# Padded copies of K for three of four segments: on-chip DMA copies of the live rows in place of VectorE multiplies, with new engine orders

## The chip, the cores and the metric

The kernel runs on one core of a Trainium2 chip. The metric is the device time of one execution in microseconds (us); lower is better. The kernel before took 261.88 us (median of three runs, 261.73 to 261.92).

## The reference, cut to what matters

One input x (2048 tokens of 512 features, bfloat16) goes through two branches that a gate mixes:

```
g   = sigmoid(sum(x * gate_w))            # one number for each token
a   = attention branch of x               # below
b   = (gelu(x @ w_gate) * (x @ w_up)) @ w_down      # inner width 1792
out = g * a + (1 - g) * b
```

The attention branch has 32 heads of width 16 and cuts the tokens into 4 segments of 512. In each segment q, k and v are x times a weight. Causal softmax attention runs inside the segment: exp(q.k / 4) with a mask, times v, divided by the row's sum. To this comes a memory read from all earlier segments: phi(q) M / (phi(q) z), where phi(t) is t + 1 for positive t and exp(t) otherwise; M sums phi(k) v and z sums phi(k) over the earlier segments. A gate per head (beta) mixes memory and attention, and wo projects the result.

## The kernel before, in words

All work is cut by segment, s = 0 to 3. K and Q are held transposed, features on the 128 partitions: `kT` and `qT` have 4 tiles of 128 features (8 heads of 16 rows each) by 512 tokens. TensorE multiplies row groups of 32 partitions, and a group of 32 holds two heads. To get the scores of one head alone, the stationary operand must be K with the other head's 16 rows set to zero. That is what `kpad[0]` and `kpad[1]` are: K with the odd, or the even, 16-row blocks of every 32 set to zero. `klow` holds pieces of K in a third layout, for the blocks at the diagonal.

Work of a segment, by task name (s is the segment, t a tile of features or of tokens):

- `K`, `Q`, `V` (tasks K1_0.0 and so on): projections on TensorE in pieces of two matmuls of 512 columns; `K1_0ev` and the like copy the result out of PSUM, on ScalarE or VectorE.
- `kp` (line 776 for segment 0, line 785 for segments 1 to 3): fills kpad from kT by a multiply with a 0/1 column on VectorE. Segments 1 to 3 have four such tasks each, `kp1_00` to `kp1_11`, each of two tiles for one j.
- `kl`: fills klow, on VectorE or ScalarE.
- `qk` (line 920): scores. For each t there are A0 and B0, which read kpad[0], A1 and B1, which read kpad[1], and for even t a block L, which reads klow. All write the same four PSUM banks X (`psXALL`), so the next one can start only when `exp` (line 926, ScalarE, 128 x 2048) has read X. GpSimd masks the result (`msk`, line 929).
- `pv` (lines 968 and 976): probabilities times V, and `pvt`, `norm` on VectorE.
- `pk` (lines 744 to 749): phi of K, written over kT in place, then `pkT`, a DMA transpose of it; `mz` (line 886) adds to the memory. `numx`, `num`, `numd`, `nump`: the memory read of a segment, whose result goes by the DMA transposes `oTd` (line 574) to oT. numx writes the X banks too, so qk of that segment waits for the last `nump`.
- `G`, `U`: gate and up projections; `gelu` (ScalarE); `Um` (line 1067): product on VectorE; `D` and `R` (line 1088): down projection and wo, the R pieces cut in four row groups; `fin`, `out`: scale and store.

TensorE runs in three ways: the whole array (line 541), four column groups of 32 (line 543, 968, 976, 886), or four row groups of 32 (lines 920, 1088, 839). A projection matmul in a stretch of the order that also has a pv task is issued as four matmuls of 32 columns (line 543) instead of one (line 541).

Each of the five queues runs its tasks strictly in the order written out in `ORDER` at the top of the file, one string for each engine; SyncE's string (`sp`) has all DMAs but the first few weights, in issue order. An emitter puts a semaphore wait in front of an instruction for each earlier writer or reader of what it touches. A waiting instruction holds all that stand behind it in its queue. The DMA helper at line 574 issues transposes, line 578 plain copies. The weights w_wu, w_wd and w_wo and the x tiles of segment 2 are held back by ticks of segment 0's exp.

The buffers that matter here: there is one kT and one pair kpad for all segments. kpad[j] of segment s may be filled only when the last qk of segment s-1 that reads it is done; phi of K writes kT, so it comes after whatever reads kT.

Of the kernel before, what the change touches and what calls it, by code (L numbers as in the profile page):

```python
# [7 lines left out]
PE, ACT, DVE, POOL, SP = "pe", "act", "dve", "pool", "sp"  # L8
# [5 lines left out]
ALU = mybir.AluOpType  # L14
# [427 lines left out]
def mm_t(n):  # L442
    return max(0.026, n / 2363.0)


def act_t(n, psum=True, ap=False):
    return (0.167 if psum else 0.20) + n / 1200.0 + (0.093 if ap else 0.0)
# [814 lines left out]
```

## Time and profile before

| | before |
|---|---|
| median of 3 runs | 261.88 us |
| profiled execution | 262.03 us, of which the span of the program 260.8 us |
| TensorE busy | 254.2 us (97%) |
| ScalarE busy | 212.4 us (81%) |
| VectorE busy | 183.8 us (70%) |
| GpSimd busy | 104.8 us (40%) |
| bytes moved by DMA | 18.43 MB |

The span runs from the first to the last instruction of the program. PE is TensorE (PEld its weight loads), DVE is VectorE, ACT ScalarE, POOL GpSimd, SP SyncE, and SPq SP's issue of DMAs. Busy is the union of an engine's instructions; a TensorE matmul overlaps the next, so that busy does not say how closely they are packed. L785 is line 785 of the file. "a <- b" in a list of waits reads: a waited until b let it go. A timeline row has its start, its length, the engine, the line, the operation and the number of instructions merged into it; "32*128" are the rows and columns of the array that a matmul uses.

### The profile page before, as it was taken

The numbers are of one execution on the slowest core, as the hardware profiler recorded it, in microseconds if no ns is written. First come the engines' busy times: TensorE is split into PE (matmuls) and PEld (weight loads), VectorE is DVE, ScalarE is ACT, GpSimd is POOL, SyncE is SP. The second block draws the span as 40 slices with busy tenths as digits, with TensorE's granted clock in tenths as the row PEclk, the third lists the DMA queues.
The fourth block names the chain that finished last, engine by engine and source line by source line (L and its number), as shares of the span: only waits on it lengthen the run. The fifth ranks groups of instructions, "written<-read, shape, count | busy, mean of one in ns | idle before, by whom it ended". The sixth has DMA issues, their size and how long they took to land.

```text
span 260.8 us, 10396 instructions
## 1 busy us (share of the span) xinstructions
PE 254.2 (97%) x4653; PEld 126.9 (49%) x4674; DVE 183.8 (70%) x348; ACT 212.4 (81%) x191; POOL 104.8 (40%) x260
## 2 busy tenths in 40 slices
PE   8999999999999999999999999999999999999996
PEld 3544354444553664534454563544455445454454
DVE  0688789989997616989889307899898301598563
ACT  4699899899999969988849867889988878877722
POOL 8206484878000544193800008548310128526430
DMA  7963263069049022190005303020000300320002
GB/s 217 318 173 61 45 186 103 3 213 195 3 49 238 14 53 63 23 124 3 3 3 120 64 5 92 15 85 1 3 4 14 93 5 0 85 64 3 3 3 83
DMA packets 32780, 18.43 MB, mean 71 GB/s; under 512 B 20576, under 2 KB 32736, under 8 KB 32736
## 3 DMA queue, kind: packets, MB, share of 16 engines
q1 hardware_dynamic: 31904, 16.99, 27.8%
q8 instruction: 36, 0.59, 0.9%
q10 hardware_dynamic: 832, 0.79, 0.9%
q14 instruction: 8, 0.07, 0.1%
HBM read 9.84 MB, written 2.10 MB: 46 GB/s over the span
## 4 chain that ended last, share of the span: by engine, by line
PE 89%; DVE 4%; ACT 2%; DMA 1%; issue 1%; POOL 0%; ACTq 0%
PE psW L541 33%; PE psW L543 24%; PE psW L1088 14%; PE psXALL L920 8%; PE psW L968 5%; PE psXALL L543 2%; DMA hT<-in_A_x_dram 1%; PE psXALL L541 1%; ACT pt L926 1%; DVE hT L564 1%; PE psW L976 1%; DVE tb L982 1%; ACT ptl L926 1%; PE psXALL L839 1%; DVE glog L814 0%
## 5 line engine op out<-in xcount | busy, mean ns | idle before, releaser
L926 ACT ACTIVATE pt<-psXALL 128x2048 bf16<-128x2048 f32 x64 | 120.1, 1877 | 25.7 <-PE psXALL L920 23.0
L929 POOL TENSOR_SCALAR_AFFINE_SELECT pt<-pt 128x256 bf16<-128x256 bf16 x128 | 57.5, 461 | 82.9 <-ACT pt L926 77.8
L929 POOL TENSOR_SCALAR_AFFINE_SELECT ptl<-ptl 128x512 bf16<-128x512 bf16 x32 | 23.1, 721 | 52.7 <-ACT ptl L926 51.0
L1067 DVE TENSOR_TENSOR hT<-psW,hT 128x512 bf16<-128x512 f32 x56 | 36.9, 682 | 9.0 <-PE psW L541 7.8
L1088 PE MATMUL psW<-wd,hT 32*128 32x512 bf16 x576 | 34.8, 374 | 0.0
L982 DVE STREAM_TRANSPOSE tb<-psW 128x512 f32<-128x512 f32 x32 | 22.3, 706 | 9.9 <-PE psW L976 9.8
L541 PE MATMUL psW<-xT,wu 128*128 128x512 bf16 x111 | 28.1, 380 | 1.2 <-issue 0.8
L1117 DVE TENSOR_SCALAR ost<-psW,omgt 128x512 bf16<-128x512 f32 x8 | 5.8, 747 | 32.7 <-PE psW L541 31.1
L541 PE MATMUL psW<-xT,wg 128*128 128x512 bf16 x112 | 28.0, 380 | 0.6 <-issue 0.3
L920 PE MATMUL psXALL<-qT,kpad 32*128 32x320 bf16 (+3 forms) x512 | 25.6, 272 | 0.4 <-ACT ptl L926 0.2
L543 PE MATMUL psW<-xT,wu 128*32 128x512 bf16 x424 | 25.9, 379 | 0.0
L543 PE MATMUL psW<-xT,wg 128*32 128x512 bf16 x432 | 25.4, 379 | 0.0
L1088 PEld LDWEIGHTS psW<-wd,hT 32*128 32x128 bf16 x576 | 18.9, 93 | 10.4
L1051 ACT ACTIVATE hT<-psW 128x512 bf16<-128x512 f32 x28 | 15.5, 596 | 6.5 <-PE psW L543 6.0
L920 PEld LDWEIGHTS psXALL<-qT,kpad 32*128 32x128 bf16 x512 | 8.8, 92 | 22.1 <-ACT pt L926 16.0
L968 PE MATMUL psW<-pt,vaug 128*17 128x192 bf16 (+3 forms) x512 | 19.2, 273 | 0.0
L541 PEld LDWEIGHTS psW<-xT,wu 128*128 128x128 bf16 x118 | 10.5, 98 | 13.6 <-issue 1.2
L541 PEld LDWEIGHTS psW<-xT,wg 128*128 128x128 bf16 x116 | 10.5, 98 | 13.0 <-issue 1.9
L968 PEld LDWEIGHTS psW<-pt,vaug 128*17 128x17 bf16 x512 | 11.8, 91 | 9.5 <-issue 0.8
L543 PEld LDWEIGHTS psW<-xT,wu 128*32 128x32 bf16 x424 | 10.9, 97 | 10.3 <-issue 0.4
L926 ACT ACTIVATE ptl<-psXALL 128x2048 bf16<-128x2048 f32 x8 | 15.0, 1880 | 1.0 <-PE psXALL L920 0.8
L543 PEld LDWEIGHTS psW<-xT,wg 128*32 128x32 bf16 x432 | 10.6, 97 | 10.1 <-issue 0.4
(124 smaller groups left out, 385.4 us busy)
## 6 DMA issues: line engine op xcount, KB each, us to landing
out_dram<-ost SPq DMA_DIRECT2D x15, 128.0 KB, 1.8
wg<-in_B_w_gate_dram SPq DMA_DIRECT2D x2, 896.0 KB, 7.2
wu<-in_B_w_up_dram SPq DMA_DIRECT2D x2, 896.0 KB, 6.8
wd<-in_B_w_down_dram SPq DMA_DIRECT2D x2, 896.0 KB, 5.9
phkt<-in_A_x_dram SPq DMA_DIRECT2D x3, 512.0 KB, 4.5
vlow<-vaug SPq DMA_DIRECT2D x8, 136.0 KB, 2.9
hT<-in_A_x_dram SPq DMA_DIRECT2D x2, 256.0 KB, 4.0
wo<-in_A_wo_dram SPq DMA_DIRECT2D x1, 512.0 KB, 6.2
```

The source lines that it names most:

```text
L541: return e.matmul(view(), lhsT, rhs, start=first, stop=last)
L543: r = e.matmul(view()[c:c + 32, :], lhsT[:, c:c + 32], rhs, start=first, stop=last, tile_position=(0, c))
L564: alts[DVE] = [Instr(lambda e: e.tensor_copy(dst(), src()), reads=reads, writes=writes, est=dve_t(n))]
L920: instrs.append(Instr(lambda e, g=g, lhs=lhs, rhs=rhs, c0=c0, ncol=ncol: e.matmul(X[g][:, c0:c0 + ncol], lhs(32 * g), rhs(32 * g), start=T ...
L926: exp_task(s, f"exp{s}_{t}{name}", [Instr(lambda e: e.activation(dst[:], XALL[:, :].rearrange("p (g c) -> p g c", g=4), ACTF.Exp, scale=AT ...
L929: task(f"msk{s}_{t}{name}", POOL, [Instr(lambda e, view=view, pat=pat, base=base: e.affine_select(out=view, in_=view, compare_op=ALU.is_ge ...
L968: instrs.append(Instr(lambda e, t=t, q=q, kb=kb, slot=slot, c0=c0: e.matmul(gp.f32()[32 * q:32 * q + 17, 128 * kb + 64:512], Vaug[sl][:, k ...
L982: task(f"pvt{s}_{t}_{j}", DVE, [Instr(lambda e: e.transpose(Tb[:, j, :], gp.f32()[:, :]), [gp.key], [("Tb", j)], 0.71)], grp=gp)
L1051: lambda e, g=g, ft=ft, s=s: e.activation(hT[s % 2][:, ft, :], g.f32()[:, :], ACTF.Gelu_apprx_tanh),
L1067: task(f"Um{s}_{ft}", DVE, [Instr(lambda e, g=g, ft=ft: e.tensor_tensor(hT[sl][:, ft, :], g.f32()[:, :], hT[sl][:, ft, :], ALU.mult), [g.k ...
L1088: return Instr(lambda e: e.matmul(gs[tile].f32()[:, :], a[32 * r:32 * r + 32, :], b[32 * r:32 * r + 32, :], start=False, stop=False, tile_ ...
L1117: DVE: [Instr(lambda e: e.tensor_scalar(ost[:], g.f32()[:, :], omgt[:, gt:gt + 1], None, ALU.mult), rd, wr, dve_t(512, ap=True))]}, grp=g))
```

## The change

Segments 1 to 3 no longer fill kpad by VectorE multiplies. Eight DMA copies for each segment, `kd1_00` to `kd1_13` and so on (j, then g), copy the 16 live rows of group g for head parity j from kT to kpad[j]: 16 partitions of 4 KB, 64 KB each. The zero rows stay as segment 0's multiplies wrote them. The dependence of kpad is kept per group of 32 rows now, so that the first matmul of each group waits for its own copy. Twelve instructions leave VectorE, 24 DMAs come to SyncE. Segment 0 is as before.

```
         if s > 0:
-            for i in range(2):
-                for j in range(2):
-                    task(f"kp{s}_{i}{j}", DVE, [Instr(lambda e, i=i, j=j: e.tensor_scalar(
-                        kpad[j][:, 2 * i:2 * i + 2, :], kT[:, 2 * i:2 * i + 2, :], maskc[j][:, 0:1], None, ALU.mult),
-                        [("kT", t) for t in (2 * i, 2 * i + 1)] + [("c", "mask", j)],
-                        [("kpad", j, t) for t in (2 * i, 2 * i + 1)], dve_t(1024, 4, ap=True))])
+            for j in range(2):
+                for g in range(4):
+                    dma(f"kd{s}_{j}{g}", SP, lambda j=j, g=g: kpad[j][32 * g + 16 * j:32 * g + 16 * j + 16, :, :],
+                        lambda j=j, g=g: kT[32 * g + 16 * j:32 * g + 16 * j + 16, :, :], [("kT", t) for t in range(4)],
+                        [("kpad", j, t, g) for t in range(4)], 65536, issue=0.47)
             klow_tasks(s, [0, 1, 2, 3])
...
-                            tile_position=(32 * g, 0)), rd, [("X", g)],
+                            tile_position=(32 * g, 0)), [k + (g,) if k[0] == "kpad" else k for k in rd],
+                            [("X", g)],
```

All five orders are written anew. Most of it is a reshuffle of the same tasks from about 17 us on; some copies out of PSUM change between ScalarE and VectorE (VectorE 348 instructions before, 334 after). The parts that the prediction speaks of:

```
pe, before: numx1 num1 K1_0.0 U0_0.0 K1_0.2 G1_8.0 G1_8.2 U0_0.2 U0_6.0 U0_6.2 U0_1.0 U0_1.2 U0_3.0 U0_3.2 U0_4.0 U0_4.2
            U0_5.0 Q2_0.0 Q2_0.2 U0_13.0 U0_7.0 U0_5.2 U0_7.2 U0_12.0 U0_13.2 U0_12.2 U0_10.0 U0_10.2 pv0_3_1 qk1_0A0
pe, after:  numx1 num1 K1_0.0 Q2_0.0 Q2_0.2 K1_0.2 G1_8.0 G1_8.2 U0_4.0 U0_3.0 U0_3.2 U0_4.2 U0_5.0 U0_1.0 U0_1.2 U0_5.2
            U0_8.0 U0_8.2 U0_10.0 U0_12.0 U0_12.2 U0_10.2 U1_0.0 U0_7.0 qk1_0A0
dve, after: numd1 nump1_0 Gev1_8 numl1 nump1_2 Um0_3 Um0_4 Um0_1 Um0_5 Um0_8 nump1_1 nump1_3 ...
act, after: exp0_3B1 Gev1_6 gelu0_0 Q2_0ev K1_0ev gelu0_2 ... gelu1_7 exp1_0A0 pke1_0 exp1_0B0 Q2_1ev Q2_3ev exp1_0L
sp, after:  x2_0 kd1_00 kd1_03 kd1_01 kd1_02 w_wo oTd1_2 kd1_10 w_wd1 oTd1_3 Vlo1_0 oTd1_0 kd1_12 kd1_13 kd1_11 x3_3 ...
            xt2 kd2_02 kd2_11 out2 kd2_03 kd2_00 x3_1 kd2_01 out1 kd2_13 kd2_10 oTd2_0 oTd2_3 oTd2_2 kd2_12 ...
            xt3 out6 out5 kd3_12 kd3_02 kd3_01 out7 kd3_11 kd3_03 kd3_00 oTd3_3 oTd3_1 kd3_10 kd3_13 ...
```

More of the change, by code (lines that the diff above doesn't have):

```diff
@@ L442, in mm_t @@
 def mm_t(n):
-    return max(0.026, n / 2363.0)
+    return max(0.026, n / 2370.0)
 def act_t(n, psum=True, ap=False):
@@ L734, in proj_T @@
                                                                    scale=maskc[0][:, 0:1]),
-                                            [key, ("c", "mask", 0)], [even[1]], act_t(512, ap=True))], grp=g)
+                                            [key, ("c", "mask", 0)], even[1], act_t(512, ap=True))], grp=g)
         copy_out(name + "ev", g, lambda: dst[:, t, :], view, [key], wkeys, 512)
@@ L772, in prep @@
             proj_T(f"K{s}_{t}", s, t, wk, "wk", kT, [("kT", t)],
-                   even=(kpad[0][:, t, :], ("kpad", 0, t)) if first else None)
+                   even=(kpad[0][:, t, :], [("kpad", 0, t, g) for g in range(4)]) if first else None)
             if s == 0:
@@ L777, in prep @@
                                                               None, ALU.mult),
-                          [("kT", t), ("c", "mask", j)], [("kpad", j, t)], 0.53)
+                          [("kT", t), ("c", "mask", j)], [("kpad", j, t, g) for g in range(4)], 0.53)
                     for j in ((1,) if first else (0, 1))])
```

156 rows, old and new, of the table ORDER are left out of this document.

## Prediction

> **What bounds the kernel now.** I read the page first, then the list of what TensorE waited for, then busy time by stretch. The page's busy row:
>
> ```profile
> span 260.8 us, 10396 instructions
> PE 254.2 (97%) x4653; PEld 126.9 (49%) x4674; DVE 183.8 (70%) x348; ACT 212.4 (81%) x191; POOL 104.8 (40%) x260
> ```
>
> TensorE is busy 254.2 of 260.8 us. Busy alone doesn't show a bound, so next all waits of TensorE that the trace shows (us in total, times, longest):
>
> ```profile
> PE psW L541 <- issue: 1.9, 12, 0.2
> PE psW L635 <- PEq L1247: 0.9, 1, 0.9
> PE psW L541 <- DVE hT L1067: 0.3, 2, 0.2
> PE psXALL L644 <- DMA hT<-in_A_x_dram: 0.3, 1, 0.3
> PE psXALL L920 <- ACT ptl L926: 0.2, 1, 0.2
> PE psW L541 <- DVE gdT L831: 0.2, 1, 0.2
> PE psW L541 <- ACT hT L561: 0.2, 1, 0.2
> PE psW L541 <- DVE tb L982: 0.2, 1, 0.2
> ```
>
> Two rows (0.9 and 0.3) are the head. One wait of 0.2 is for an exp. The other 17 are all in front of line 541, the whole-array form, 2.8 us in total, 0.16 each, whatever engine is named. They come where TensorE goes back from row groups to the whole array; I price them below. So after the head no engine makes TensorE wait visibly. VectorE, which the change relieves, stands in the way nowhere in this list.
>
> Third, the three stretches between one segment's attention and the next, where the removed instructions are (columns: stretch, then busy us of PE, PEld, DVE, ACT, POOL):
>
> ```profile
> 59.00:78.00 19.00, 19.00 (x420) 9.73 (x421) 18.25 (x39) 18.94 (x13) 4.99 (x21) 1.00 0.49 77
> 125.00:140.00 15.00, 14.84 (x298) 7.43 (x298) 13.52 (x31) 10.43 (x17) 4.35 (x16) 1.00 0.10 24
> 190.00:204.00 14.00, 13.84 (x338) 7.14 (x332) 12.47 (x31) 11.97 (x19) 0.15 (x1) 1.00 0.10 21
> L785 DVE TENSOR_SCALAR kpad<-kT,maskc x12: 388/477/487, 55.8 to 227.1; 128x1024 bf16<-128x1024 bf16 x12
> ```
>
> VectorE is 90% busy or more there, but TensorE 99 to 100%. TensorE bounds these stretches too.
>
> **The change part by part.**
>
> *TensorE's work.* The same matmuls remain. The changed order splits fewer of them into four column groups (4503 instructions against 4674). That is worth nothing:
>
> ```profile
> 160.17 2.27 PE psW L541 x10
> 129.31 5.35 PE L543 MATMUL psW<-xT,wg 128*32 128x512 bf16 x96
> 134.49 0.61 PE L968 MATMUL psW<-pt,vaug 128*17 128x448 bf16 x16
> ```
>
> Ten whole matmuls take 2.27 us on the chain, one entry included, so about 0.216 each; 96 quarter matmuls start at 129.31 and the next form at 134.49: 5.18 / 24 = 0.216 for four.
>
> *Changes of form.* Both orders have 124 changes between whole array, row groups and column groups: 81 to or from whole arrays and 43 between rows and columns before, 85 and 39 after. Two forms of return to the whole array cost differently:
>
> ```profile
> 137.00 0.40 PE L920 MATMUL psXALL<-qT,kpad 32*128 32x448 bf16 x8
> 137.55 1.24 PE L541 MATMUL psW<-xT,wg 128*128 128x512 bf16 x5 [0.16 <-issue]
> 157.18 0.40 PE L920 MATMUL psXALL<-qT,kpad 32*128 32x320 bf16 x8
> 157.51 1.04 PE L541 MATMUL psW<-wv,xT 128*128 128x512 bf16 x4
> ```
>
> The same block of 512 columns (0.216 us) takes 0.55 us to the next start at 137.00 and 0.33 at 157.18: a short change is 0.11, a long one 0.22 more. Following the timeline, the 17 long ones are the 11 returns with column groups before the row groups, the three after a whole R stretch, and three others that I can't explain. The changed order has 12 and three of the first two kinds: one more, **+0.22 us**; the three others I keep.
>
> *VectorE.* Twelve instructions by 467 ns (5.6 us of its 183.8) go. All lie beside a saturated TensorE: **0**. If TensorE weren't the bound, a stretch would gain up to 4 x 0.47 = 1.9 us.
>
> *The copies.* 24 issues on SyncE. No SBUF-to-SBUF copy of 16 partitions is in the trace; the nearest rows (KB each, median us from issue to landing) and issue lengths:
>
> ```profile
> vlow<-vaug SPq DMA_DIRECT2D x8, 136.0 KB, 2.9
> wd<-in_B_w_down_dram SPq DMA_DIRECT2D x2, 896.0 KB, 5.9
> out_dram<-obf SPq DMA_DIRECT2D x1, 32.0 KB, 1.5
> 78.41 0.62 SPq L578 DMA_DIRECT2D vlow<-vaug  x1
> 75.51 1.49 SPq L578 DMA_DIRECT2D wd<-in_B_w_down_dram  x1
> 77.05 1.25 SPq L574 DMA_TRANSPOSE oT<-phkt  x1
> ```
>
> I take 0.6 us of issue and 2.9 to land, as vlow has (also on chip); the ends are 1.5 and 5.9. Against the consumers, segment 1 first, from these rows:
>
> ```profile
> 61.71 0.24 PE L543 MATMUL psW<-mzbd,phq 128*32 128x136 bf16 x4
> 62.03 1.09 DVE L851 TENSOR_SCALAR ndsc<-psXALL,exr 128x32 f32<-128x32 f32 x4
> 63.42 0.95 DVE L858 RECIPROCAL ndsc<-ndsc 128x128 f32<-128x128 f32 x1
> 63.64 0.58 ACT L561 ACTIVATE kT<-psW 128x512 bf16<-128x512 f32 x1
> 73.66 0.40 PE L920 MATMUL psXALL<-qT,kpad 32*128 32x448 bf16 x8
> 84.72 0.39 PE L920 MATMUL psXALL<-qT,kpad 32*128 32x448 bf16 x8
> ```
>
> - The last kT tile was out of PSUM at 64.22; in the new order one copy of 0.6 stands ahead of it: 64.8. The four kd1_0 issue from there, the last starts at 64.8 + 3 x 0.6 = 66.6 and lands at 69.5 (68.1 to 72.5). Their reader, qk1_0A0, stands 22 pieces behind num: 61.77 + 22 x 0.432 = 71.3. Margin 1.8 us (73.66 is its start before, with 26 pieces and a pv).
> - The same block also needs the last nump. From numd's end at 64.37 the new order has four nump (0.65), one copy (0.69), numl (0.29) and five Um (0.69): 64.37 + 7.0 = 71.4. So TensorE comes and is let go at the same time; I put **+0.1** for it (0 to 0.4).
> - The kd1_1 stand behind oTd1_2, which waits for that nump: 71.4, then three transposes of 1.25, w_wd1 (up to 1.5), Vlo (0.6) and four copies (0.6): the last starts at 79.9 and lands at 82.8, at most 5.9 later, 85.8. Reader: the A1 block, 84.72 before, and no earlier now (a phi of 1.05 is put ahead of it on ScalarE). Margin 1.9 us at my value, minus 1.1 at the far end.
> - phi of K writes kT and now waits for the copies. Behind it on VectorE stand the second phi and three scale-and-stores that wait for D (84 us and later): nothing that is due.
> - Segments 2 and 3, from the last qk of the segment before and the first of segment 3:
>
> ```profile
> 123.50 0.40 PE L920 MATMUL psXALL<-qT,kpad 32*128 32x320 bf16 x8
> 186.51 0.40 PE L920 MATMUL psXALL<-qT,kpad 32*128 32x320 bf16 x8
> 202.29 0.40 PE L920 MATMUL psXALL<-qT,kpad 32*128 32x448 bf16 x8
> ```
>
>   The copies may start after 123.9 and 186.9, and the order has kT complete by about then; I allow 2 us more. Four kd_0 with other issues between them end within 5 us and land 2.9 later: 134 and 197, against qk at 137.00 and 202.29. The kd_1 behind oTd, from about 137 and 201, land within 9 us; A1 comes three blocks behind the first qk, over 9 us later. Hidden, with the thinnest margin at 137.00 (3 us).
>
> The Trainium skill, "DMA: Bandwidth & Descriptors", section Bandwidth, speaks against this: "Batch DMAs to ≥1 MiB for ≥75% of peak. Transfers under 64 KB are descriptor-dominated", with 0.95 us of DMA time for 64 KB. By that figure, as an estimate, the four kd1_0 would be spaced by 0.95 instead of 0.6 and the last land near 70.6, still ahead of its reader, and the sum would be the same. No row of this trace has such a copy.
>
> *First matmuls with a wait each.* Six qk blocks now wait for four semaphores, one for each row group, all long set. Bounds: 0; and the spread that the chain shows for qk blocks of 8, 0.33 to 0.40:
>
> ```profile
> 73.73 0.33 PE psXALL L920 x8
> 79.51 0.40 PE psXALL L920 x8
> ```
>
> I take half: 6 x 0.035 = **+0.2** (0 to 0.4).
>
> *The rest of the new order.* Exp blocks end the weight loads' idle time of qk:
>
> ```profile
> PEld psXALL L920 <- ACT pt L926: 17.7, 43, 0.6
> PEld psXALL L920 <- ACT ptl L926: 2.6, 6, 0.7
> ```
>
> Mean 17.7 / 43 = 0.41, about what a change of form leaves anyway; the longest, 0.6 and 0.7, show some 0.3 us lost in each of a few blocks, perhaps 1 us in all. A new order loses these anew or not: **-0.3** taken, from -1.0 to +1.0, as it may lose as much again.
>
> *Sum*, against the profiled execution (262.03): 0.22 + 0.1 + 0.2 - 0.3 = +0.2, so 262.25. It ran 0.15 above the median of the runs (261.88), so **262.1 us**. Its own bounds add up: -1.0 at best, 0.22 + 0.4 + 0.4 + 1.0 = +2.0 at worst; 260.9 to 263.9.
>
> **The rivals.**
>
> 1. *Late copies (slower).* SyncE works in order, and kd1_1 stands behind a w_wd1 of 896 KB and a transpose that waits for VectorE. If those copies land as w_wd does (5.9) the A1 block of segment 1 starts at 85.8 instead of 84.7; with a nump 1 us late besides, 2 us are lost. Price 1 to 2 us, 263 to 264. It decides from a landing later than 84.7. Against it: the vlow row, 2.9. The same at kd1_0 needs over 4.7 us.
> 2. *The order fits worse (slower).* Without any DMA: where the order puts too little between two qk, or one copy too many on ScalarE between two exps, TensorE runs dry; the rows on L920 above show that 0.3 a block is possible. Four such blocks more than before: +1.2, 263.1.
> 3. *The freed VectorE helps (faster).* If what TensorE loses hangs on late VectorE work (PSUM banks freed late at 90% busy), the new order could recover the 1 us and one or two of the long changes: 1.0 + 0.4 against the +0.5 above, 260.9 to 261.2. Against it: the list of TensorE's waits names VectorE four times, 0.7 us, and these are changes of form.
> 4. *The copies don't replace anything on the critical path* is the forecast itself; that they don't do what they say is excluded, the instructions of line 785 are gone from the built program.
>
> **How the numbers follow.** Two medians of this kernel can be told apart from about 0.2% (0.52 us): faster is below 261.36, slower above 262.40. The forecast (262.1, own range 261.4 to 262.4 without its far ends) gets 0.47; late copies 0.14, a worse order 0.18, and 0.21 for the faster side, which has rival 3 and the lucky end of the order's term. Slower 0.32. The range leaves out about a tenth on each side: 261.1 to 263.5.
>
> **What would show each step right or wrong.** Of the changed kernel's profile: TensorE busy still 96 to 98%; some 18 waits of line 541 of 0.16 us; VectorE busy lower by about 5 us, plus what moves to it from ScalarE; kd copies that land in 2 to 3.5 us; no wait of L920, on TensorE or its weight loads, whose releaser is the DMA kpad<-kT. The forecast is wrong if such a wait appears (rival 1), if the waits of L920 for exp grow by over 1 us (rival 2), or if those 17 long changes shrink to well under 14 (rival 3).

## The result and the profile after

The changed kernel takes 263.18 us (median of 6 runs, 262.73 to 264.00) against 261.85 us for the kernel before (6 runs, 261.68 to 262.03). The ratio is 1.0056 with an interval of 1.0040 to 1.0073: slower by half a per cent, 1.33 us. The profiled execution took 263.11 us with a span of 261.9, 1.1 more than before. Of all the runs below one, of e3, was disturbed (658 us) and is left out.

Three rows of the changed kernel's page, the span, the busy times and the issue of its copies:

```profile
span 261.9 us, 10074 instructions
...
PE 255.0 (97%) x4481; PEld 126.5 (48%) x4503; DVE 179.8 (69%) x334; ACT 213.4 (82%) x191; POOL 104.9 (40%) x260
...
kpad<-kT SPq DMA_DIRECT2D x24, 64.0 KB, 2.4
```

VectorE is relieved by 4.0 us and TensorE is still busy 97%. The copies land in 2.4 us (median). All that TensorE waited for by the trace, and in a second list two rows of its weight loads (us in total, times, longest):

```profile
PE psW L541 <- issue: 2.5, 16, 0.2
PE psW L635 <- PEq L1247: 0.9, 1, 0.9
PE psW L968 <- DVE hT L564: 0.3, 1, 0.3
PE psXALL L644 <- DMA hT<-in_A_x_dram: 0.3, 1, 0.3
PE psXALL L919 <- ACT ptl L926: 0.2, 1, 0.2
PE psW L541 <- DVE mzc L899: 0.2, 1, 0.2
```

```profile
PEld psXALL L919 <- ACT pt L926: 15.1, 38, 0.4
...
PEld psXALL L919 <- DMA kpad<-kT: 0.4, 1, 0.4
```

The rows on line 541 are no waits, as the next part shows. Of the others two are new. A pv (line 968) waits 0.3 us for an eviction on VectorE, and one score block waits 0.4 us for a copy. The score blocks' waits for exp did not grow: 15.1 us in all, 17.7 before. The chain of waits of the changed kernel, cut from 54 to 86 us, shows where both rows stand (start, us, what):

```profile
54.59 0.59 DVE glog L813
55.19 0.61 DVE hT L564
55.79 0.04 issue
55.84 0.61 PE psW L968 x16
...
62.31 0.17 PE psW L541
62.48 0.05 issue
62.53 9.59 PE psW L541 x43
...
78.05 0.02 SPq L434
78.06 0.04 issue
78.10 0.68 SPq L578
...
78.83 2.25 SPq L574
...
82.39 3.78 DMA kpad<-kT
86.17 0.05 issue
86.21 0.21 PE psXALL L919
```

At 54.59 the chain leaves TensorE and runs over VectorE. The new order has two gate sums (line 813) ahead of the eviction Gev0_0 (line 564) there, and the pv task pv0_2_0 needs the bank which that eviction frees. At 78 us it runs over SyncE: a copy of V to vlow (78.10), transposes (78.83), the last three kd1_1 copies, and the last of these lands at 86.17. What held SyncE until 78 is a row of SyncE's own waits, and what the late copy did to the block stands in the timeline:

```profile
SPq L434 <- PE psW L976: 2.7, 1, 2.7
```

```profile
85.79 0.79 PE L919 MATMUL psXALL<-qT,kpad 32*128 32x448 bf16 x5
86.21 0.12 PEld L919 LDWEIGHTS psXALL<-qT,kpad 32*128 32x128 bf16 x7 [0.36 <-DMA kpad<-kT]
```

The copy Vlo1_0 overwrites what the last pv of segment 0 reads. Before, the two pv0_3 stood next to qk1_0A0, one on either side; the new order puts both behind ten more tasks. So Vlo1_0 waits 2.7 us, and three kd1_1 copies behind it wait as well. The block A1 of segment 1 starts at 85.79 with the one row group whose copy is there and stands still until 86.21.

**Where the time is lost.** To compare kernels with different orders I count each trace's matmuls as work (512 columns on the whole array 0.216 us, the same in a column or row group a quarter of it) and ask when each kernel has done as much as the kernel before at a given time. For this the records must be complete, and they are not: the pages have 4674 weight loads (PEld) but 4653 matmuls before, 4503 and 4481 after. One of the places is the return to the whole array that the prediction shows at 137.55, with five matmuls. The loads there, and those of the "short" return that it shows at 157.51 with four matmuls:

```profile
137.32 0.98 PEld L541 LDWEIGHTS psW<-xT,wg 128*128 128x128 bf16 x6 [0.21 <-issue]
```

```profile
157.51 0.55 PEld L541 LDWEIGHTS psW<-wv,xT 128*128 128x128 bf16 x4 [0.21 <-DVE ost L1117]
```

A piece has two matmuls, so three pieces are six, and the first of them has no record. It would start at 137.33, as the first does at 157.51, and take 0.216 us, up to the next start at 137.55; that fills the "wait" of 0.16. So it is at all 17 long returns before and at 18 places after (the other four missing records of each kernel lie in the first 28 us). With a matmul counted for each load, a return to the whole array costs 0.10 to 0.15 us beyond the work wherever it stands, and the rows on line 541 (2.8 us before, 2.7 after) are no idle time. There are no long returns.

The table counts the loads without a matmul as matmuls. All fourteen traces then hold the same work, 237.27 us. The delay in us, less that at 11.6 us (the head, which varies from run to run, see the end); the figures are good to about 0.05:

| kernel | head | 57.3 | 65.9 | 83.0 | 91.1 | 135.4 | 222.7 |
|---|---|---|---|---|---|---|---|
| changed kernel | -0.11 | 0.65 | 0.79 | 0.67 | 1.14 | 1.13 | 1.22 |
| e0, the same again | -0.11 | 0.65 | 0.78 | 0.66 | 1.50 | 1.48 | 1.58 |
| e1, copies ahead | +0.54 | 0.64 | 0.77 | 0.65 | 0.72 | 0.71 | 0.81 |
| e2, new orders, multiplies | +0.55 | 0.64 | 0.69 | 1.05 | 1.10 | 1.01 | 1.04 |
| e3, old orders, copies | 0.00 | 0.08 | 0.08 | 0.16 | 0.22 | 0.28 | 0.48 |
| d1, copies nobody reads | -0.32 | 0.00 | 0.00 | 0.00 | 0.00 | 0.00 | -0.02 |
| d2, neither copies nor multiplies | -0.08 | 0.01 | 0.00 | 0.00 | 0.00 | 0.00 | -0.02 |
| h1, old start, new rest | -0.03 | 0.08 | 0.82 | 0.70 | 0.76 | 0.80 | 0.89 |
| h1b, h1 with the seam mended | +0.29 | 0.08 | 0.57 | 0.52 | 0.58 | 0.62 | 0.71 |
| h1c, h1b with multiplies | +0.24 | 0.01 | 0.64 | 1.06 | 1.11 | 1.02 | 1.04 |
| h2, new start, old rest | -0.25 | 0.64 | 0.70 | 0.77 | 0.83 | 0.91 | 1.14 |
| m1, two places mended | -0.11 | 0.08 | 0.26 | 0.52 | 0.52 | 0.56 | 0.65 |
| m2, three places mended | -0.39 | 0.08 | 0.27 | 1.50 | 1.56 | 1.59 | 1.69 |

The first line reads: 0.79 us are lost by 66 us, before any copy of the change is read; 0.47 between 83 and 91 us, where the held block stands (e1, without the hold, loses 0.07 there); and little after that. The parts of the first 66 us, by the gaps between matmul starts beyond their work and a change of form: 0.28 in two places at 32.9 and 33.5 us, 0.08 at 42.0, 0.33 at the pv of 55.84, and 0.14 at 65.05.

### The profile page after: what moved, and what is told of

The parts are those of the page before. It is cut to its first block, busy times and chain, and to the rows that moved or that the text cites. A ratio compares the mean times of both kernels' runs of the same rounds, so it can differ in the third digit from the quotient of the medians.

```text
span 261.9 us, 10074 instructions
## 1 busy us (share of the span) xinstructions
PE 255.0 (97%) x4481; PEld 126.5 (48%) x4503; DVE 179.8 (69%) x334; ACT 213.4 (82%) x191; POOL 104.9 (40%) x260
## 4 chain that ended last, share of the span: by engine, by line
PE 88%; DVE 4%; DMA 3%; SPq 2%; ACT 1%; issue 1%; ACTq 0%
PE psW L541 37%; PE psW L543 19%; PE psW L1088 14%; PE psXALL L919 8%; PE psW L968 5%; PE psXALL L543 2%; DMA kpad<-kT 1%; DMA hT<-in_A_x_dram 1%; PE psW L976 1%; PE psXALL L541 1%; DVE hT L564 1%; SPq L574 1%; ACT pt L926 1%; ACT ptl L926 1%; SPq L578 1%
## 5 line engine op out<-in xcount | busy, mean ns | idle before, releaser
L929 POOL TENSOR_SCALAR_AFFINE_SELECT pt<-pt 128x256 bf16<-128x256 bf16 x128 | 54.1, 433 | 134.3 <-ACT pt L926 129.5
L541 PE MATMUL psW<-xT,wu 128*128 128x512 bf16 x157 | 38.9, 379 | 0.8 <-issue 0.6
L541 PE MATMUL psW<-xT,wg 128*128 128x512 bf16 x110 | 27.4, 379 | 0.5 <-issue 0.5
L1117 DVE TENSOR_SCALAR ost<-psW,omgt 128x512 bf16<-128x512 f32 x9 | 6.4, 748 | 28.6 <-PE psW L541 27.0
L929 POOL TENSOR_SCALAR_AFFINE_SELECT ptl<-ptl 128x512 bf16<-128x512 bf16 x32 | 24.4, 763 | 2.9 <-ACT ptl L926 1.3
L541 PEld LDWEIGHTS psW<-xT,wu 128*128 128x128 bf16 x162 | 14.7, 98 | 19.0 <-issue 1.9
L825 POOL COPY exsT<-exs 32x4 f32<-32x4 f32 x64 | 14.9, 233 | 6.2 <-ACT exs L816 2.4
L543 PE MATMUL psW<-xT,wu 128*32 128x512 bf16 x248 | 15.7, 380 | 0.0
```

The source lines that it names most:

```text
L541: return e.matmul(view(), lhsT, rhs, start=first, stop=last)
L543: r = e.matmul(view()[c:c + 32, :], lhsT[:, c:c + 32], rhs, start=first, stop=last, tile_position=(0, c))
L825: cross = task(f"exsT{s}", POOL, [Instr(lambda e, g=g, c=c: e.tensor_copy(exsT[sl][32 * g:32 * g + 32, c:16:4], exs[32 * c:32 * c + 32, s4 ...
L929: task(f"msk{s}_{t}{name}", POOL, [Instr(lambda e, view=view, pat=pat, base=base: e.affine_select(out=view, in_=view, compare_op=ALU.is_ge ...
L1117: DVE: [Instr(lambda e: e.tensor_scalar(ost[:], g.f32()[:, :], omgt[:, gt:gt + 1], None, ALU.mult), rd, wr, dve_t(512, ap=True))]}, grp=g))
```

## The experiments

The kernel before ran beside each group of these (e0 to e3; h1, h2, d2 and m1; h1b, h1c and d1; m2), with medians of 261.98, 261.94, 262.01 and 261.96 us. The ratios are those of the means, so they can differ from the quotient of the medians by some hundredths of a per cent.

**e0. The changed kernel once more**, unaltered.

> The changed kernel again, beside the three that take it apart, for its spread on this chip. Both theories: a median of 263.0 to 263.4 (263.18 in six runs). The profiled run lost 0.38 us at the A1 block of segment 1, where a copy landed at 86.17. If that loss depends on when the copy lands (theory 1, the copies held up in SyncE's queue), the runs spread by about 1 us, and another profile shows another loss there. If the loss is in the fixed order of segment 0 and elsewhere (theory 2), single runs should spread no more than those of before (0.35 us).

Measured: 263.44 us (262.98 to 263.82), ratio 1.0052 (1.0039 to 1.0066). The result stands, a little above the range. In this execution A1 of segment 1 waits longer for its copy:

```profile
PE psXALL L919 <- DMA kpad<-kT: 0.5, 1, 0.5
```

The copy's landing varies, and with it the loss at this place: 0.47 in one profile, 0.84 in the other (1.50 less 0.66 in the table). That the runs spread (0.84 us) decides nothing between the theories, since e1 spreads by more.

**e1. Copies ahead.** The new orders; in SyncE's, three copies move:

```
-oTd1_2 kd1_10 w_wd1 oTd1_3 Vlo1_0 oTd1_0 kd1_12 kd1_13 kd1_11 x3_3
+oTd1_2 kd1_10 kd1_12 kd1_13 kd1_11 w_wd1 oTd1_3 Vlo1_0 oTd1_0 x3_3
```

> The changed kernel with one edit of SyncE's order: kd1_12, kd1_13 and kd1_11 stand right behind kd1_10, ahead of w_wd1, of two transposes and of Vlo1_0, which waited 2.7 us for pv0_3. Theory 1 (these copies are late because they stand behind a waiting DMA): the last of them lands near 78 instead of 86, the wait of L919 for kpad<-kT is gone, the time falls by 0.4 us or more, to 262.2 to 262.8, and the spread shrinks to some 0.3. Theory 2 (the rest of the new order): within 0.2 us of the changed kernel, same spread.

Measured: 263.03 us (262.77 to 264.47), ratio 1.0044 (1.0028 to 1.0060). Its timeline of SyncE and of the weight loads:

```profile
74.02 1.85 SPq L574 DMA_DIRECT2D kpad<-kT  x3
```

```profile
86.38 0.15 PEld L915 LDWEIGHTS psXALL<-qT,kpad 32*128 32x128 bf16 x8 [0.31 <-issue]
```

The copies issue by 75.9, seven microseconds earlier, the block runs through, and no row of its waits has kpad<-kT as releaser. The place is mended: the delay goes from 0.65 to 0.72 past it, not to 1.14 or 1.50. But only 0.15 to 0.41 us of the median goes (against 263.18 and 263.44); 1.05 us above the kernel before remain, and the spread is no smaller. The time misses the range of the theory of late copies, which explains the smaller part.

**e2. The new orders with VectorE's multiplies.** No copies; the twelve `kp` tasks are put into VectorE's new order behind the same neighbours as before, as far as it allows:

```
-kd1_00 ... kd3_13                       (SyncE, 24 copies)
+kp1_10 ... kp3_11                       (VectorE, 12 multiplies)
```

> The new orders of the changed kernel, but kpad of segments 1 to 3 made by the twelve VectorE multiplies again, put in at about the places they had before; no copies. Theory 1: the loss at A1 of segment 1 is gone, the two waits of pv in segment 0 (0.18 and 0.43 us) stay, and 5.6 us come back to VectorE beside TensorE: 262.4 to 262.9. Theory 2: 263.0 to 263.5, as the changed kernel. If VectorE in the stretches between attentions is what limits (rival 3 of the prediction), it is clearly slower, by up to 1.9 us a stretch: above 264.

Measured: 263.03 us (262.91 to 263.94), ratio 1.0045 (1.0030 to 1.0059). The new orders lose 1.05 us without any copy, and at 57 and 66 us the table has the delay of the changed kernel within 0.01 and 0.10. The chain of this kernel has the same gate sums and the same eviction ahead of the pv:

```profile
54.64 1.19 DVE glog L810 x2
55.83 0.61 DVE hT L560
56.44 0.04 issue
56.48 0.61 PE psW L965 x16
```

A further 0.34 us, at qk1_0A0 (72.67 us), are of my making: a multiply stands ahead of a nump that the block waits for. So e2's 1.05 us are more than the orders themselves cost; by e1's trace, with the copies in time, it is 0.8.

**e3. The old orders with copies.** The orders of the kernel before without the multiplies; the eight copies of a segment in one go, behind w_wo, x3_0 and xt3:

```
-w_wo oTd1_0
+w_wo kd1_00 kd1_01 kd1_02 kd1_03 kd1_10 kd1_11 kd1_12 kd1_13 oTd1_0     (likewise kd2, kd3)
```

> The orders of the kernel before, without the twelve multiplies, and with the copies: kd1 all eight behind w_wo, kd2 behind x3_0, kd3 behind xt3, each as soon as kT is complete. Theory 1: the copies then land 4 us or more before their readers, nothing waits, and the time is that of before, 261.7 to 262.0: the copies themselves cost nothing, nor does the relief of VectorE bring anything. Theory 2 says the same of this one. If a wait of its own for each row group costs (0.2 us in the prediction, at most 0.4), 262.0 to 262.3; if VectorE limits, below 261.4.

Measured: 262.56 us (ten runs, 262.31 to 263.41), ratio 1.0022 (1.0013 to 1.0031). That is outside every range above: less than the changed kernel loses, but more than nothing, though SyncE issues eight copies without a gap and the last lands at 71 us, 13 us ahead of A1:

```profile
64.41 5.02 SPq L573 DMA_DIRECT2D kpad<-kT  x8
```

Matched with the kernel before matmul by matmul (4653 in the same order), the delay comes in six steps of 0.06 to 0.15 us: at 56.0, 79.7, 84.9, 123.8, 174.4 and 211.6 us. Two of them, 0.06 at 84.9 and 0.09 at 211.6, are blocks whose row groups wait for copies. The second of these is in the new orders too: near 211 us e1's delay grows from 0.72 to 0.81, and that of e2, without copies, not at all. The other four are not such blocks; d1 and d2 go after them.

**d2. Neither copies nor multiplies.** The old orders without the twelve tasks. The score blocks of segments 1 to 3 read segment 0's padded K: that part of the computation is left out.

> The orders of the kernel before; the twelve multiplies of segments 1 to 3 are gone and no copies take their place, so that the score blocks of segments 1 to 3 read the padded K of segment 0 (this part of the computation is left out). Theory A (VectorE's 6 us lie beside TensorE's work): within 0.2 us of the kernel before, 261.8 to 262.1. Rival R (a freed VectorE answers TensorE sooner): 261.0 to 261.5. What the old orders with copies (262.6 against 262.0) lie above this run is the price of copies and of waiting for them: 0.5 to 0.7 by theory A.

Measured: 261.98 us (261.69 to 262.49), ratio 1.0002 (0.9992 to 1.0011). On its page VectorE is relieved and TensorE the same to the tenth:

```profile
PE 254.2 (98%) x4653; PEld 127.5 (49%) x4674; DVE 179.8 (69%) x336; ACT 212.5 (82%) x191; POOL 103.8 (40%) x260
```

From 8 us to the end the 4653 matmuls start as in the kernel before less a constant 0.07 to 0.11 us. The relief of VectorE is worth nothing in these orders, and the 0.6 us of e3 come with the copies.

**d1. Copies that nobody reads.** The kernel before with its multiplies, and the copies of e3 besides, into off-chip scratch:

```
+kdum = nc.dram_tensor("kdum", (P, 4, 512), BF, kind="Internal").ap()
-dma(f"kd{s}_{j}{g}", ... kpad[j][32 * g + 16 * j: ...], ... [("kpad", j, t, g) ...])
+dma(f"kd{s}_{j}{g}", ... kdum[32 * g + 16 * j: ...], ... [("kdum", j, t, g) ...])
```

> The kernel before with its multiplies, and besides them the 24 copies at the places of the run with old orders and copies, but into off-chip scratch memory that nothing reads, so that no score block waits for a copy; SyncE still issues them, and VectorE's in-place update of K still waits for them. Theory W (what the copies cost is the waiting of the score blocks, three steps of 0.06 to 0.09 us in the trace, and a few of the same kind): 262.0 to 262.2 us. Theory Q (it is SyncE's queue and VectorE's waits): 262.4 to 262.6, as with the copies that are read.

Measured: 261.83 us (261.67 to 262.58), ratio 0.9996 (0.9987 to 1.0005). The page has 24 copies that land in 2.2 us:

```profile
kdum<-kT SPq DMA_DIRECT2D x24, 64.0 KB, 2.2
```

The time is a little below theory W's range and clear of theory Q's: issue on SyncE and reading kT cost nothing. What is left for e3's price is that the copies write kpad and that blocks wait for them and read it; d1, whose copies go off the chip and whose blocks read what multiplies wrote, doesn't tell these apart. The same block's weight loads in e3 (first fence) and in d1:

```profile
84.91 0.15 PEld L914 LDWEIGHTS psXALL<-qT,kpad 32*128 32x128 bf16 x8 [0.36 <-issue]
```

```profile
84.37 0.13 PEld L922 LDWEIGHTS psXALL<-qT,kpad 32*128 32x128 bf16 x8 [0.30 <-ACT ptl L929]
```

The gap is 0.06 longer with a releaser that the trace can't name, although the copy had landed 13 us before. For the four steps elsewhere I found no cause. They are in e3, the first also in h1 and h1b, and none of them is in d1 or d2. The first, 0.08 at 56.0, comes through ScalarE, whose exp ahead of the block starts at 54.11 instead of 54.02, ten microseconds before the first copy is issued. So neither the writing nor the reading of copies can be its cause.

**h1. Old start, new rest.** Every engine runs the old order up to num1 (62 us), the new one from there; copies as in e3 for segment 1, as in the changed kernel for the others.

> The copies stay; every engine runs the order of the kernel before up to the end of segment 0 (TensorE up to num1 at about 62 us, the other engines up to the same moment) and the new order from there; all eight copies for segment 1 are issued in one go behind the weight load w_wo. Theory A (the new orders lose their time before 66 us, where the trace of the changed kernel is already 1.1 us behind at equal TensorE work, and next to nothing later): the start comes back, the held block at 86 us too, and what is left is the waits of the row groups, some 0.2 us; 262.1 to 262.4 us against some 262.0 for the kernel before. Rival B (the loss is spread over the segments, and the later ones only make it look early): at most a third comes back, 262.8 to 263.1. Theory C (the copies themselves cost half a microsecond wherever they stand): 262.5 to 262.7.

Measured: 262.84 us (262.62 to 263.16), ratio 1.0036 (1.0023 to 1.0048), a miss. The table says why: 0.08 at 57.3 us, as hoped, and then one loss of 0.74 at the seam, after which next to nothing more is lost. The time lies in rival B's range, but not for rival B's reason. The chain there:

```profile
54.17 8.77 DMA xT<-in_A_x_dram
62.93 0.05 issue
62.98 3.20 PE psW L537 x14
```

The new order has Q2_0 right behind num1, and the x tile that it reads was loaded for the old order's later Q2_0.

**h1b. The seam mended.** Q2_0 goes where the old order has it:

```
-num1 K1_0.0 Q2_0.0 Q2_0.2 K1_0.2 G1_8.0 G1_8.2 U0_4.0 U0_3.0 U0_3.2 U0_4.2 U0_5.0 U0_1.0
+num1 K1_0.0 K1_0.2 G1_8.0 G1_8.2 U0_4.0 U0_3.0 U0_3.2 U0_4.2 U0_5.0 Q2_0.0 Q2_0.2 U0_1.0
-gelu0_0 Q2_0ev K1_0ev gelu0_2 gelu0_6 gelu0_10
+gelu0_0 K1_0ev gelu0_2 gelu0_6 Q2_0ev gelu0_10
```

> The old start and the new rest again, with the seam mended: there the second segment's query projection Q2_0 came right behind num1, and TensorE waited 0.57 us for its x, whose load the old order issues later. It goes behind U0_5.0 now, as in the kernel before, and its eviction behind gelu0_6. Theory A (the new orders lose only in their first 66 us): 262.84 less some 0.7: 262.1 to 262.4 us, against 261.95 for the kernel before. Rival B (the later part of the new orders loses by itself): 262.6 or more.

Measured: 263.18 us (262.51 to 264.02), ratio 1.0038 (1.0023 to 1.0053), a miss again. The wait for x is gone and another has come:

```profile
PE psW L537 <- ACT kT L557: 0.3, 1, 0.3
```

The next projection now waits for K1_0's bank, and the stretch from 57 to 66 us loses 0.49 instead of 0.74. From 66 us on the new orders lose little here either (0.57, at the end 0.71). The medians don't show the gain: 1.17 us above the kernel before here, 0.90 for h1.

**h1c. The same with multiplies** in place of the copies.

> The same orders with VectorE's twelve multiplies put back at the places that the kernel before gives them, and no copies. If waiting for the copies costs a few tenths in any order (0.6 us was measured with the old orders, next to nothing with the new ones): 261.8 to 262.1 us, no faster than the kernel before by more than 0.2. If the copies cost nothing in this order: the same as the run with the seam mended, or slower by what the multiplies hold up (up to 0.4).

Measured: 263.06 us (262.93 to 263.56), ratio 1.0040 (1.0028 to 1.0053). The seam costs 0.63 here, and another 0.42 goes by 83 us. So it doesn't tell what copies cost in this order; the medians of h1b and h1c don't differ measurably.

**h2. New start, old rest**, the new orders up to num1, then the old ones with the copies of e3.

> The reverse: the new order on every engine up to num1, then the order of the kernel before without its multiplies, the copies of segments 1 to 3 issued early. Theory A: all of the new orders' loss is kept, and the row groups' waits come on top: 263.0 to 263.4 us. Rival B: most of the loss goes: 262.4 to 262.7, as with the old orders throughout and the copies.

Measured: 263.01 us (262.88 to 263.35), ratio 1.0042 (1.0029 to 1.0054), as theory A had it: 0.70 at 66 us is kept to the end, and the rest adds 0.44, as in e3 (0.40 from there).

**m1. Two places mended** in the orders of e1:

```
-Gev1_4 gsum1_3 gsum1_1 Gev0_0 gsum1_0          (VectorE)
+Gev1_4 Gev0_0 gsum1_3 gsum1_1 gsum1_0
-V1_0.0 pv0_0_0 V1_0.2                          (TensorE)
+V1_0.0 V1_0.2 pv0_0_0
```

> The changed kernel with the copies of segment 1 issued ahead, and two places of segment 0 mended: the eviction Gev0_0 goes ahead of two gate sums in VectorE's order (TensorE waits 0.33 us for its bank at 55.8 us), and pv0_0_0 goes behind V1_0.2 on TensorE (0.18 us at 33.5 us). Theory A: half a microsecond less than with the copies ahead alone (263.0): 262.4 to 262.7. Rival B (single waits do not add up, the next bank is as late): 262.9 to 263.1.

Measured: 262.61 us (262.01 to 263.44), ratio 1.0027 (1.0013 to 1.0041), in the range of theory A. The pv no longer waits; the timeline has it right behind the one before:

```profile
54.60 0.61 PE L964 MATMUL psW<-pt,vaug 128*17 128x448 bf16 x16
55.04 0.29 PE L972 MATMUL psW<-ptl,vlow 128*17 128x64 bf16 x16
55.16 0.61 PE L964 MATMUL psW<-pt,vaug 128*17 128x448 bf16 x16
```

The delay is 0.08 instead of 0.64 at 57.3 us and 0.26 instead of 0.77 at 65.9. In this execution 0.36 is lost again in the block at 83.1 us, where the trace names no releaser.

**m2. A third place mended**, on top of m1:

```
-U1_0.0 U0_7.0 qk1_0A0 ... U0_9.0 U0_9.2 pv0_3_1 pv0_3_0       (TensorE)
+U1_0.0 U0_7.0 pv0_3_1 qk1_0A0 ... U0_9.0 U0_9.2 pv0_3_0
-Um0_7 Um1_4 Um0_11 Um0_2 Um0_9 gts0 pvt0_3_0 pvt0_3_1         (VectorE)
+Um0_7 pvt0_3_1 Um1_4 Um0_11 Um0_2 Um0_9 gts0 pvt0_3_0
```

> The kernel with two mended places (262.61 us) and a third: pv0_3_1 goes ahead of qk1_0A0 again, as in the kernel before, so that the stretch from num1 to qk1_0A0 has a pv in it and runs in column groups instead of the whole array. In the trace of the changed kernel that stretch pays a return to the whole array behind num1 (62.53 us, 0.23) and 0.14 at 65.05, neither of which the kernel before has. Its eviction pvt0_3_1 goes behind Um0_7. Theory A (the new orders' loss is a sum of such places in the first 66 us): 262.2 to 262.4 us against 261.95 for the kernel before, and at equal TensorE work the trace is within 0.5 us of it at 66 us. Rival B (what is mended in one place turns up in another): 262.5 or more.

Measured: 263.90 us (263.52 to 264.73), ratio 1.0077 (1.0058 to 1.0096), the slowest of all. At the place itself nothing was to be gained: the 0.23 of the expectation is a matmul without a record (the changed kernel has two weight loads of xT,wk from 62.26 on and one matmul, at 62.53), and the 0.14 is still there, now at 64.25. The delay at 65.9 us is 0.27, as in m1 (0.26). Then about 0.3 is lost at the pv that was moved and 1.04 behind the block. The row of TensorE's waits, then the chain:

```profile
PE psW L539 <- DVE hT L1063: 0.9, 1, 0.9
```

```profile
72.50 1.44 PE psW L539 x24
...
73.96 0.02 DVEq L430
73.98 0.04 issue
74.03 0.70 DVE hT L1063
74.73 0.04 issue
74.77 1.25 PE psW L539 x17
```

VectorE stood idle until 74.03 for the second half of U1_0, which TensorE has five tasks behind the first. By the orders two results that were complete, Um0_7's and the moved pv's, stood behind that eviction on VectorE with their banks; TensorE ran out of banks and got its next one when the eviction was done, at 74.77. Each engine was held by the other's place in its order. Rival B was right here: what is mended in one place turned up in the next.

## Why the prediction was right and wrong, by its steps

The time fell into the range, but not into the likeliest case: I forecast no measurable change (0.47), and the kernel is slower by 1.33 us (0.32).

- **The step that failed: "the rest of the new order", taken as -0.3 (-1.0 to +1.0).** e2 has the new orders alone at +1.05 us, 0.34 of it by a multiply that I placed badly, and e1, without the held copy, has 0.78 at the end of its trace. The sign was wrong, and so was the place where I looked. I read the rows in which score blocks wait for exp, and those waits shrank from 17.7 to 15.1 us. The loss lies in segment 0, in tasks that the change's words don't mention: a PSUM bank that VectorE frees late because gate sums stand ahead of an eviction, and a pv that stands one task too early. h2 keeps the start's 0.64 with the old rest, h1 and h1b have 0.08 at 57 us with the old start, and m1 took out 0.5 us by two moves. That the list of waits before named VectorE hardly at all said that the old order fits, not that any order would.
- **Late copies (rival 1), in part.** It named the place and the sign, and its sign appeared: a wait for kpad<-kT, with a landing later than 84.7. Of the working for kd1_1 the issue of Vlo failed: I priced it at its 0.6 us of issue and missed its wait of 2.7 us for pv0_3, which the new order had moved far behind qk1_0A0. The last copy was due at 82.8 (at most 85.8; the terms as written add up to 0.85 less), landed at 86.17, and the price was 0.42 us by the traces of the changed kernel and e1, 0.15 to 0.41 by their medians, not 1 to 2.
- **The order fits worse (rival 2).** Its price of 1.2 us is near what e2 shows, and it got 0.18. Its mechanism, too little between two qk or one copy too many between two exps, didn't happen.
- **The freed VectorE helps (rival 3): fell.** d2 takes the multiplies away, and no matmul moves by more than 0.04 us. The 0 in the sum was right, and for the reason given. VectorE's busy time fell by 4.0 us there and in the changed kernel, not by 5.6.
- **One more long return (+0.22): wrong, it is 0.** The gaps that I read as long returns are matmuls without a record, 17 before and 18 after. The 0.22 is the time of one matmul, and the explanations by column groups and R stretches fitted by chance. The busy row that I showed had the sign of it, 4674 weight loads and 4653 matmuls. So TensorE has no waits on line 541 to be freed of, in either kernel.
- **A wait for each row group (+0.2): about right in size for what can be placed, 0.15,** at two of the six blocks in e3. Another 0.33 of e3's delay goes with the copies, at places I can't explain. With the new orders e1 and e2 have the same median, and e1's trace is 0.23 shorter; but e2 has its badly placed multiply, so this doesn't settle whether copies in time cost more than well-placed multiplies.
- **The tie at qk1_0A0 (+0.1): 0.** The block starts without a gap. e2 shows that it was close: one multiply ahead of the nump costs 0.34.
- **The other copies: hidden, as predicted.** Only one score block waits for a copy. They issue 0.6 us apart and land in 2.4 (predicted 2.9, bounds 1.5 and 5.9). By the 0.95 us for 64 KB in "DMA: Bandwidth & Descriptors", section Bandwidth, of the Trainium skill, which was measured for loads from HBM to 128 partitions, eight of them would take 7.6 us (an estimate). In e3 eight on-chip copies issue in 5.0 us and the last lands 2.4 after its start. The measurement decides.

That the measured time fell into the range was luck in part: the range was wide enough for an order term of the wrong sign. Two things are shown: the new orders alone cost 0.8 (e1's trace) to 1 us (medians of e1 and e2), nearly all before 66 us, and the held copy 0.2 to 0.4 more by the medians, 0.4 and 0.8 in the two traces. Open are the four small steps that come with the copies, and whether the start of the new orders could be mended to the end: m1 got two thirds of it by 66 us and lost 0.36 again at 83, and m2 found nothing at its place and lost more behind it. No version here measurably beats the kernel before; with TensorE's work unchanged and VectorE's share hidden, d2 bounds what removing the multiplies can bring in these orders at nothing.

## What to carry to other kernels

When an edit comes with orders made anew, price the orders as a change of their own: read each engine's new sequence for evictions that have moved behind work nobody waits for, over the whole program and not only at the edited place. For each DMA in a queue, price what it waits for as well as its issue, since all that stands behind it inherits the wait. And when an engine's relief is to bring time, leave its work out altogether first: if no matmul moves, nothing that replaces the work can gain. Before an idle time in front of matmuls is priced, compare the number of matmuls in the profile with that of weight loads: a gap as long as one matmul may be a matmul without a record.

## What the runs showed of the hardware that I had not expected

- The first matmuls run at half pace for a time that differs between runs. The same eight of 128 columns, which start 0.056 us apart in the changed kernel from the third on and 0.106 apart in e1:

```profile
4.50 0.65 PE L644 MATMUL psXALL<-ident,hT 128*128 128x128 bf16 x8 [0.28 <-DMA hT<-in_A_x_dram]
```

```profile
4.51 1.03 PE L640 MATMUL psXALL<-ident,hT 128*128 128x128 bf16 x8 [0.30 <-DMA hT<-in_A_x_dram]
```

  In e1 this puts the whole execution 0.65 us later than the changed kernel's. A single profile's span can't be compared below that; the delay behind the head can.
- Behind the head an execution repeats itself to a few hundredths: d2 and d1 follow the kernel before over some 250 us within 0.04 us, though one has twelve instructions fewer and the other 24 DMAs more.
- The kernels with new orders scatter more (262.73 to 264.00 for the changed kernel) than the kernel before (261.68 to 262.03 beside it; 261.66 to 262.59 beside the experiments, and once 263.08). The landing of the held copy is one cause (0.47 and 0.84 us lost at its block); e1, which has no such hold, scatters by 1.7 us as well, and there the cause stays open.
